# GpSimd's bonus products in two instructions of four heads, and W_in's casts over an even number of outer columns, in a recurrence-and-MLP kernel

## The chip, the cores and the metric

The kernel runs on one core of one Trainium2 chip. The metric is the time of one execution in microseconds on the device, as the median of several runs of the same kernel. TensorE (PE in the profile), VectorE (DVE), ScalarE (ACT) and GpSimd (POOL) compute, each going through its own list of instructions in order; SyncE (SP) issues nearly all DMAs.

## What is computed

A linear recurrence over 768 steps is followed by a two-layer MLP. B = 4, H = 8 heads, S = 768 steps, D = 48 per head, so a token has H*D = 384 numbers, and the hidden layer has 2048.

```python
for t in range(S):
    kt, vt, rt, wt = k[:, :, t], v[:, :, t], r[:, :, t], w[:, :, t]
    cur = np.einsum('bhd,bhe->bhde', u[None] * kt, vt)
    y[:, :, t] = np.einsum('bhd,bhde->bhe', rt, state + cur)
    state = wt[:, :, :, None] * state + np.einsum('bhd,bhe->bhde', kt, vt)
...
x = y.transpose(0, 2, 1, 3).reshape(B * S, H * D)
h = x @ w_in
return np.maximum(0.01 * h, h) @ w_out
```

The part of `cur` that concerns us is the bonus: for each token and head, the sum over d of r*u*k is one number, and it multiplies the token's v.

## The kernel before, in words

The 3072 tokens are cut into 24 chunks of 128 tokens (`NCH`; tokens lie on the 128 partitions), 6 chunks for each batch. The chunks of a batch hang together through the state; the MLP of a chunk needs only that chunk's y. Chunks 0 to 3 go in two pairs (`pair`, L537), the others one by one (`single`, L714).

For each chunk the four inputs w, k, r, v (128 x 384, f32) are loaded into a buffer of the ring `in` (L516). ACT takes the logarithm of w (`lw`, L383), TensorE sums it over time (`cp`, L737), DVE adds to it (`ci`, L752), and ACT takes exponentials (`ek` and, in place, `cp`, L393). The products `rk` (k*ek and r*exp(cp), bf16) are made by DVE or POOL through the helper `times` at L334. They are turned to `rkT`: by TensorE and a copy up to chunk 11 (L441, copies at L329 and L331), by a DMA transpose from chunk 12 on (`TDMA`, L431). TensorE multiplies them to scores `se`, `so` (L787), DVE masks them (`m`, L459), TensorE makes `yp` from m and v (L822) and from the scaled state `sb` (L817). The state `s` is DVE's sum (L479) of `sb`, a product through L334, and of TensorE's outer products of k and v (L640 for pairs, L798).

The bonus (`bonus`, L402 to L421) has four steps: `ru` = r*u, `ru` = ru*k (both mostly on POOL, L334), a sum over each head on DVE to `dg` with 8 numbers for a token (L416), and `vs` = v*dg, in which each number is spread over its head's 48 columns. This last product is 128 x 384 f32 in one instruction of 8 heads, on POOL for 19 chunks and on DVE for 5 (L334 again). `vs` is read in one place: `finish` (L490), where DVE adds it to yp and gives `y`. y goes to `xT`, by TensorE and a copy (L504) or by a DMA transpose (L496).

The MLP of a chunk: TensorE multiplies W_in's 384 x 2048 and xT in four steps of 12 matmuls into `hp` (L860), ACT applies the leaky ReLU and writes `g` (L907), TensorE multiplies g and W_out into `op` in four steps of four matmuls (L928), ACT or DVE copies it to `o` (L329 or L331), and SP stores it (L968).

The weights come as f32 and are cast to bf16 on chip once (`weight_steps`, L349). W_in comes in four buffers, each in two halves: three blocks of 128 rows (t) by 256 columns, so that the f32 half is one contiguous run of 768 for each partition, and its place in `w_in_b` is three runs of 256, 2048 apart. W_out likewise comes in four buffers of two halves, whose place is four runs of 192. Each half is one DMA on SP (L363) and one cast (`copy`, L327: ACT at L329, DVE and POOL at L331). Five of W_in's eight casts are on ACT, two on POOL and one on DVE; of W_out's, two are on ACT, four on POOL and two on DVE.

All steps are recorded with an estimated duration and dependencies (`step`, L317; class `Plan`). A list written out by hand (`EARLY`, L162) gives every step its rank and, by a letter, for some steps another engine (a, v, p for ACT, DVE, POOL). For each compute engine the listed steps also depend on the one ranked before them on that engine, so that the order on each engine stands as written (L972 to L984). The step's function gets the chosen engine as its argument `e`. `P0` is ten times the chunk's number, so `P0 >= 120` means chunk 12 and later.

Of the kernel before, what the change touches and what calls it, by code (L numbers as in the profile page):

```python
# [126 lines left out]
def kernel(  # L127
# [12 lines left out]
    B, H, S, D = r.shape  # L140
# [19 lines left out]
    CASTS = 21  # L160
# [103 lines left out]
    with tc.manual_schedule():  # L264
# [29 lines left out]
        for q in (0, 64):  # L294
            for i, op in ((slice(0, 64), ALU.is_gt), (slice(64, 128), ALU.is_gt),
                          (slice(128, 192), ALU.is_ge), (slice(192, 256), ALU.is_gt)):
                t = pmask[q : q + 64].rearrange("p a t -> p (a t)")[:, i]
# [19 lines left out]
        def step(eng, dur, fn, pri, reads=(), writes=(), deps=(), wire=None, rows=0, **alts):  # L317

            d = list(deps)
            for x in writes:  # L320
                d += x.old
            i = plan.add(eng, dur, fn, d, pri, wire, rows, {eng: dur, **alts} if alts else None)
            for x in (*reads, *writes):
                x.steps.append(i)
            return i

        def copy(e, o, i):  # L327
            if e == "ACT":
                nc.scalar.copy(out=o, in_=i)  # L329
            else:  # L330
                (nc.vector if e == "DVE" else nc.gpsimd).tensor_copy(out=o, in_=i)  # L331

        def times(e, o, a, b):
            (nc.vector if e == "DVE" else nc.gpsimd).tensor_tensor(out=o, in0=a, in1=b, op=ALU.mult)  # L334
# [10 lines left out]
        win_s, wout_s = [], []  # L345
        JQ = NJ // NQ


        def weight_steps(q, which, pri):  # L349
            st = in_r.take()  # L350

            made = []
            for half in range(2):
                part = st.t[:, half * 768 : (half + 1) * 768].rearrange("p (t f) -> p t f", t=(KT, JQ)[which])
                if which == 0:
                    f0 = q * 512 + half * 256
                    src, dst = w_in_v[:, :, f0 : f0 + 256], w_in_b[:, :, f0 : f0 + 256]
                else:
                    n0 = half * DM // 2
                    src = w_out_v[:, q * JQ : (q + 1) * JQ, n0 : n0 + DM // 2]  # L360
                    dst = w_out_b[:, q * JQ : (q + 1) * JQ, n0 : n0 + DM // 2]
                ld = step(
                    "SP", 0.45, lambda part=part, src=src: nc.sync.dma_start(out=part, in_=src), pri,  # L363
                    writes=[st], wire=WWIRE[which], rows=(384, 512)[which])
                made.append(step(
                    ("DVE", "ACT")[half], (0.8, 0.84)[half],
                    lambda e, dst=dst, part=part: copy(e, dst, part), CASTS, reads=[st], deps=[ld],
                    DVE=0.8, ACT=0.84, POOL=1.2))
            (win_s if which == 0 else wout_s).append(made)

# [25 lines left out]
        def product(rk, a, xn, e, P0, deps, banked):  # L396
# [2 lines left out]
                lambda eng: times(eng, rk.t[:, a, :, 0:D], xn.t, e.t[:]),  # L399
                P0, reads=[xn, e], writes=[rk], deps=deps, **({"DVE": 0.58} if banked else {"POOL": 1.05}))  # L400

        def bonus(vs, rn, kn, vn, loads, P0):  # L402

            ru, dg = ru_r.take(), dg_r.take()
            kl, rl, vl = loads
            s_ru = step(
                "POOL", 1.05,
                lambda e: times(e, ru.t[:], rn.t, ubv),
                P0 + 2, reads=[rn], writes=[ru], deps=[rl, u_ld], DVE=0.84)
            s_ruk = step(  # L410
                "POOL", 1.05,
                lambda e: times(e, ru.t[:], ru.t[:], kn.t),
                P0 + 2, reads=[kn, ru], deps=[kl, s_ru], DVE=0.84)
            s_dg = step(
                "DVE", 0.54,
                lambda: nc.vector.tensor_reduce(out=dg.t[:], in_=ru.t[:], axis=AX.X, op=ALU.add),  # L416
                P0 + 2, reads=[ru], writes=[dg], deps=[s_ruk])
            return step(
                "POOL", 0.92,
                lambda e: times(e, vs.t[:], vn.t, dg.t[:].unsqueeze(2).to_broadcast([128, H, D])),  # L420
                P0 + 2, reads=[vn, dg], writes=[vs], deps=[vl, s_dg], DVE=0.84)  # L421

        def gt(t):
# [108 lines left out]
        def weights_at(n):  # L532
            for i, (at, pri) in enumerate(WEIGHTS):
                if n == at:
                    weight_steps(i % NQ, i // NQ, pri)

        def pair(n):  # L537
# [89 lines left out]
            for j in range(2):  # L627
                s_T += turn(rk[j], rkT[j], s_d[j], n, P0, (hp_r, hp_r) if j and n == 0 else (se_r, so_r))
            vs = [vs_r.take() for _ in range(2)]
            s_vs = [bonus(vs[j], rn[j], kn[j], vn[j], (kl, rl, vl), P0) for j in range(2)]  # L630


# [81 lines left out]
        def single(n):  # L714
# [48 lines left out]
            s_T = turn(rk, rkT, [s_r, s_k], n, P0, (se_r, so_r))  # L763
            vs = vs_r.take()
            s_vs = bonus(vs, rn, kn, vn, (kl, rl, vl), P0)


# [115 lines left out]
        for nb in range(4, len(blocks) + 1):  # L883
            a = made[nb][0] if nb < len(blocks) else []
# [12 lines left out]
        for rank, (kind, nb, item) in enumerate(seq):  # L897
            pri = 1000 + rank
            if kind == 0:
                up, j, J, N, g, m_chs, deps = item  # L900
# [17 lines left out]
            else:  # L918
# [12 lines left out]
                deps = [g_done[nb, j] for j in range(q * NJ // 4, (q + 1) * NJ // 4)]  # L931
                deps += wout_s[q * NJ // 4 // JQ] + ([downs[ch]] if q else [])
                if (ch, q) == (NCH - 1, 3):

                    for part, (t, n0, n1) in enumerate(last_parts(op)):
                        o = o_r.take()
# [23 lines left out]
                if q == 3:  # L960
                    o = o_r.take()
                    s_o = step(
                        *(("ACT", 0.5) if ch < OACT else ("DVE", 0.56)),
                        lambda e, o=o, op=op: copy(e, o.t[:], op.t[:, 0:DM]),
# [11 lines left out]
        for rank, word in enumerate(EARLY.split()):  # L976
            i = int(word.rstrip("avp"))
# [50 lines left out]
```

## Time and profile before

| | us |
|---|---|
| median of 5 runs | 186.16 |
| lowest and highest of them | 185.93 and 186.78 |
| the profiled execution's own time | 186.78 |
| its span, first to last instruction | 184.7 |
| TensorE busy | 176.1 (95%) |
| TensorE's weight loads busy | 137.2 (74%) |
| DVE, ACT, POOL busy | 121.2, 121.3, 93.0 |
| `vs` on POOL | 19 instructions, 16.1 in all |
| `vs` on DVE | 5 instructions, 3.0 in all |
| W_in's casts: ACT, POOL, DVE | 0.832 (5), 0.824 (2), 0.953 (1) each |
| W_out's casts: ACT, POOL, DVE | 0.832 (2), 0.824 (4), 0.560 (2) each |

The profile is of one execution. A line of a group gives the source line, the engine, the operation, what it writes and reads, the number of instructions, their busy time and the mean of one in ns, then how long the engine sat idle just before them and what ended that idle time. A line of a timeline gives the start and the duration in us. "PEld" is TensorE's weight load, which overlaps its matmuls. Matmuls are pipelined: a matmul of 128 columns is shown with 219 ns, though they follow each other much more closely. All products of `times` have the line L334, and so are told apart by the names of their tiles.

### The profile page before, as it was taken

What the parts mean: (1) busy time and instruction counts of PE and PEld (TensorE: products, weight loads), DVE (VectorE), ACT (ScalarE), POOL (GpSimd) and SP (SyncE); (2) the same over time, 40 slices, a digit from 0 to 9 for tenths busy, and PEclk for the clock granted to TensorE, in tenths of its full rate; (3) what the DMA queues carried; (4) which work ended last, traced back from release to release, by engine and by line L of the source; (5) the groups of instructions that cost most, each with busy time, mean ns of one, the idle gap of its engine ahead of it and who ended that gap; (6) DMA issues with size and microseconds to landing.
All of it is one profiled execution on the core that took longest, in us unless ns stands there. A gap on an engine that the chain in (4) does not pass through costs nothing.

```text
span 184.7 us, 6227 instructions
## 1 busy us (share of the span) xinstructions
PE 176.1 (95%) x2579; PEld 137.2 (74%) x2583; DVE 121.2 (66%) x237; ACT 121.3 (66%) x263; POOL 93.0 (50%) x129
## 2 busy tenths in 40 slices
PE   7987799999999999999999999999999999999992
PEld 2465587777788697788687787886978777877882
DVE  2488585358678877987868778658548588755000
ACT  2784966665786987798958586666557646652660
POOL 7987582552466778889165656313516256110000
PEclk9999999999999999999999999999999999999999
DMA  6999999988989998996885998888986998941202
GB/s 146 261 282 316 348 330 277 250 172 204 222 166 245 196 230 197 229 217 140 172 159 109 118 199 180 206 163 158 191 203 146 200 197 216 152 108 39 66 4 85
DMA packets 120238, 34.62 MB, mean 187 GB/s; under 512 B 109841, under 2 KB 120210, under 8 KB 120210
## 3 DMA queue, kind: packets, MB, share of 16 engines
q1 hardware_dynamic: 120208, 34.22, 84.1%
q8 instruction: 20, 0.33, 0.8%
q14 instruction: 8, 0.07, 0.1%
q10 hardware_dynamic: 2, 0.00, 0.0%
HBM read 25.17 MB, written 4.72 MB: 162 GB/s over the span
## 4 chain that ended last, share of the span: by engine, by line
PE 77%; SPq 10%; DMA 8%; POOL 2%; issue 1%; DVE 0%
PE op L928 31%; PE hp L860 31%; SPq L516 5%; SPq L363 5%; DMA in<-in_moe_w_in_dram 5%; DMA in<-in_moe_w_out_dram 3%; PE se L787 3%; PE yp L822 2%; PE cp L737 2%; PE yp L817 2%; PE yp L798 2%; PE so L441 1%; PE se L441 1%; PE yp L504 1%; PE cp L742 1%
## 5 line engine op out<-in xcount | busy, mean ns | idle before, releaser
L907 ACT ACTIVATE g<-hp 128x512 bf16<-128x512 f32 x96 | 56.7, 596 | 35.8 <-PE hp L860 33.9
L860 PE MATMUL hp<-xT,w_in_b 128*128 128x128 bf16 x1152 | 76.2, 219 | 1.5 <-ACT w_in_b L329 0.9
L860 PEld LDWEIGHTS <-w_in_b 128*128 128x128 bf16 x1152 | 67.4, 98 | 6.5 <-ACT w_in_b L329 1.2
L928 PE MATMUL op<-w_out_b,g 128*128 128x384 bf16 (+1 forms) x380 | 71.4, 324 | 0.2 <-DVE w_out_b L331 0.2
L928 PEld LDWEIGHTS <-g 128*128 128x128 bf16 x392 | 34.9, 98 | 17.7 <-DVE w_out_b L331 0.3
L334 POOL TENSOR_TENSOR ru<-in,ub 128x384 f32<-128x384 f32 x19 | 19.0, 1007 | 11.7 <-DMA in<-in_r_dram 8.4
L334 POOL TENSOR_TENSOR rk<-in,ek 128x384 bf16<-128x384 f32 x15 | 15.2, 1011 | 17.0 <-ACT ek L393 15.6
L334 POOL TENSOR_TENSOR vs<-in,dg 128x384 f32<-128x384 f32 x19 | 16.1, 852 | 14.5 <-DVE dg L416 11.3
L490 DVE TENSOR_TENSOR y<-yp,vs 128x384 bf16<-128x384 f32 x24 | 13.3, 555 | 13.0 <-PE yp L822 9.5
L334 POOL TENSOR_TENSOR ru<-ru,in 128x384 f32<-128x384 f32 x15 | 15.5, 1042 | 4.1 <-DMA in<-in_k_dram 2.5
L334 POOL TENSOR_TENSOR sb<-s,a 128x384 bf16<-128x384 f32 x13 | 11.3, 867 | 11.7 <-DVE s L479 4.4
L459 DVE TENSOR_TENSOR m<-se,maskb 128x512 bf16<-128x512 f32 x20 | 13.7, 685 | 3.6 <-PE so L787 3.3
L459 DVE TENSOR_TENSOR m<-so,maskb 128x512 bf16<-128x512 f32 x20 | 13.7, 685 | 3.5 <-PE so L787 3.5
L383 ACT ACTIVATE lw<-in 128x384 bf16<-128x384 f32 x24 | 12.3, 520 | 3.1 <-DMA in<-in_w_dram 3.1
L752 DVE TENSOR_TENSOR ci<-cp,lw 128x384 f32<-128x384 f32 x20 | 11.1, 553 | 4.3 <-PE cp L742 3.9
L334 DVE TENSOR_TENSOR rk<-in,cp 128x384 bf16<-128x384 f32 x22 | 12.1, 548 | 2.6 <-ACT cp L393 2.1
L416 DVE TENSOR_REDUCE dg<-ru 128x8 f32<-128x384 f32 x24 | 13.0, 545 | 0.2
L329 ACT COPY o<-op 128x384 f32<-128x384 f32 (+1 forms) x16 | 7.5, 470 | 6.5 <-PE op L928 5.1
L479 DVE TENSOR_TENSOR s<-yp,sb 128x384 f32<-128x384 f32 x14 | 7.8, 554 | 5.2 <-PE yp L798 5.2
L393 ACT ACTIVATE cp<-cp 128x384 f32<-128x384 f32 x22 | 10.5, 479 | 0.6 <-DVE ci L752 0.3
L393 ACT ACTIVATE ek<-ci 128x384 f32<-128x384 f32 x20 | 10.4, 518 | 0.4 <-DVE ci L752 0.2
L441 PEld LDWEIGHTS <-rk 128*128 128x128 bf16 x96 | 6.6, 103 | 2.4 <-DVE rk L334 1.0
(125 smaller groups left out, 222.9 us busy)
## 6 DMA issues: line engine op xcount, KB each, us to landing
out_dram<-o SPq DMA_DIRECT2D x23, 192.0 KB, 2.9
in<-in_w_dram SPq DMA_DIRECT2D x20, 192.0 KB, 4.1
in<-in_r_dram SPq DMA_DIRECT2D x20, 192.0 KB, 3.7
in<-in_k_dram SPq DMA_DIRECT2D x20, 192.0 KB, 3.9
in<-in_v_dram SPq DMA_DIRECT2D x20, 192.0 KB, 3.7
in<-in_moe_w_in_dram SPq DMA_DIRECT2D x8, 384.0 KB, 7.7
in<-in_moe_w_out_dram SPq DMA_DIRECT2D x8, 384.0 KB, 7.4
in<-in_w_dram SPq DMA_DIRECT2D x2, 384.0 KB, 5.0
```

The costliest lines, as they stand in the source:

```text
L334: (nc.vector if e == "DVE" else nc.gpsimd).tensor_tensor(out=o, in0=a, in1=b, op=ALU.mult)
L363: "SP", 0.45, lambda part=part, src=src: nc.sync.dma_start(out=part, in_=src), pri,
L383: lambda: nc.scalar.activation(out=lw.t[:, :, 0:D], in_=wn.t, func=AF.Ln),
L393: "ACT", 0.5, lambda: nc.scalar.activation(out=out.t[:], in_=i, func=AF.Exp, scale=scale),
L416: lambda: nc.vector.tensor_reduce(out=dg.t[:], in_=ru.t[:], axis=AX.X, op=ALU.add),
L441: nc.tensor.transpose(trv[:, g, :], rk.t[:, a, 2 * g : 2 * g + 2, :].rearrange("p h d -> p (h d)"), ident[:])
L459: lambda par=par: nc.vector.tensor_tensor(out=m.t[:, par], in0=gt(sc[par].t), in1=mask.unsqueeze(1).to_broadcast([128, NP, 128]), op=ALU.m ...
L490: lambda: nc.vector.tensor_tensor(out=y.t[:], in0=hd(yp.t[:, 0:DM]), in1=vs.t[:], op=ALU.add),
L752: lambda: nc.vector.tensor_tensor(out=ci.t[:], in0=hd(cp.t[:, 0:DM]), in1=lw.t[:, :, 0:D], op=ALU.add),
L860: nc.tensor.matmul(hp.t[:, a * N : (a + 1) * N], lhsT=w_in_b[:, t, (j + a) * 128 : (j + a + 1) * 128], rhs=xT[:, t, c0 : c0 + N], start=(a ...
L907: lambda hp=hp, g=g, j=j, J=J, N=N: nc.scalar.activation(out=g.t[:, j : j + J, 0:N], in_=hp.t[:, 0 : J * N].rearrange("p (a n) -> p a n", ...
L928: nc.tensor.matmul(t[:, 0 : n1 - n0], lhsT=g.t[:, j, off : off + 128], rhs=w_out_b[:, j, n0:n1], start=(j == 0), stop=(j == NJ - 1))
```

## The change

Two independent edits. In `weight_steps`, the cast of a half of W_in is given another view of the same elements: each run of 256 columns is split in two halves of 128, and the half (a) becomes the outermost dimension, so that source and destination both have 2 x 3 rows of 128 in place of one run of 768 and three rows of 256. All eight casts of W_in are affected, on whichever engine they are; W_out's are left as they were. In `bonus`, where the last product is on POOL and the chunk is 12 or later, it is made in two instructions of four heads (128 x 192) each, one after the other. These are nine of the nineteen on POOL, those of chunks 12, 14, 16 and 18 to 23. On every engine the order of the instructions is otherwise the same.

```diff
+        def even(t, which):
+
+            return t if which else t.rearrange("p t (a f) -> p a t f", a=2)
...
-                    lambda e, dst=dst, part=part: copy(e, dst, part), CASTS, reads=[st], deps=[ld],
+                    lambda e, dst=even(dst, which), part=even(part, which): copy(e, dst, part), CASTS, reads=[st], deps=[ld],
...
+        def by_heads(e, o, a, b, parts):
+            for i in range(parts):
+                hs = slice(i * H // parts, (i + 1) * H // parts)
+                times(e, o[:, hs, :], a[:, hs, :], b[:, hs].unsqueeze(2).to_broadcast([128, H // parts, D]))
...
-                lambda e: times(e, vs.t[:], vn.t, dg.t[:].unsqueeze(2).to_broadcast([128, H, D])),
+                lambda e: by_heads(e, vs.t, vn.t, dg.t, 2 if e == "POOL" and P0 >= 120 else 1),
```

## The prediction, as it was made before the changed kernel ran

> **What bounds the kernel now.** I read the page first: the 40 slices say where each engine is full.
>
> ```profile
> PE 176.1 (95%) x2579; PEld 137.2 (74%) x2583; DVE 121.2 (66%) x237; ACT 121.3 (66%) x263; POOL 93.0 (50%) x129
> ...
> PE   7987799999999999999999999999999999999992
> ...
> DMA  6999999988989998996885998888986998941202
> ```
>
> TensorE is at 9 from slice 8 on (a slice is 184.7 / 40 = 4.62 us); before that the DMA row is full and TensorE isn't. So there are two stages, and I cut the span at 40.4 us, where the chain of waits becomes TensorE alone, and asked for busy times by window:
>
> ```profile
> 18.00:40.40 22.40, 20.20 (x393) 16.37 (x387) 13.43 (x25) 15.27 (x28) 12.89 (x16) 1.00 1.01 279
> 40.40:181.40 141.00, 141.00 (x1983) 112.41 (x1981) 96.29 (x178) 95.16 (x211) 65.75 (x74) 1.00 0.81 168
> ```
>
> The columns are the window and its length, then PE, PEld, DVE, ACT, POOL with counts, then clock, DMA share, GB/s. In the second window TensorE is busy for all 141.00 of 141.00 us. Asked who waited for whom from 40.5 to 181.4 us, TensorE has no entry at all. A busy TensorE need not be at its peak, but nothing here waits for DVE, ACT or POOL. From 18 to 40.5 us it has these:
>
> ```profile
> PE hp L860 <- ACT w_in_b L329: 0.9, 2, 0.6
> PE so L441 <- POOL rk L334: 0.5, 1, 0.5
> PE hp L860 <- ACT g L907: 0.4, 1, 0.4
> PE op L928 <- DVE w_out_b L331: 0.2, 1, 0.2
> ```
>
> (total us, times, longest): 2.0 us together. The reader should notice what isn't there: DVE's cast of W_in. The last of these waits, the 0.5 at about 40 us, is what fixes where the full stage begins, and the chain shows what it hangs on:
>
> ```profile
> 31.39 6.39 DMA in<-in_moe_w_out_dram
> 37.78 0.05 issue
> 37.84 0.57 POOL w_out_b L331
> 38.41 0.43 issue
> 38.83 1.10 POOL rk L334
> 39.94 0.05 issue
> 39.98 0.40 PE so L441 x4
> ```
>
> The last piece of W_out lands at 37.78; POOL, idle 1.46 us before, casts it, forms rk, and TensorE goes on at 39.98. The front is paced by the weights' arrival, and the SP queue that issues those loads goes by the DMA engines (share 1.01), not by the engines of this change. The loads into reused buffers that also wait for POOL or DVE (25.49 and 28.97 us) wait for products of chunks 0 and 1, done by 14 us.
>
> [...] a cast of 768 elements whose destination has 4 outer columns against one of 3:
>
> ```profile
> 20.79 0.95 DVE L331 CAST w_in_b<-in 128x768 bf16<-128x768 f32 x1 [1.70 <-DMA in<-in_moe_w_in_dram]
> 21.66 0.41 DVE L331 COPY rkT<-so 128x512 bf16<-128x512 bf16 x1
> ...
> 28.92 0.56 DVE L331 CAST w_out_b<-in 128x768 bf16<-128x768 f32 x1 [1.64 <-DMA in<-in_moe_w_out_dram]
> ```
>
> [...] DVE's sb at 23.38, started under POOL's cast of 23.07 to 23.89, took 0.92 in place of 0.55. [...] POOL's casts give the size: 822 ns for 768 elements, 502 for 384, so 0.83 ns an element and about 0.18 us fixed.
>
> **Part 1, the casts of W_in.** There are eight: five on ACT (832 ns), two on POOL (824), one on DVE (953). Same elements, now in 2x3 rows of 128; the order on every engine is unchanged.
> DVE: 953 becomes 560, the row of the 4-column cast: 0.39 us less. [...] The rkT copy behind it reads transposes issued at 20.90, so it can follow. TensorE's outer products, which wait for that copy, stand behind twelve hp matmuls of 21.41 to 22.1 that wait for an xT copy on ACT. There is no DVE wait in TensorE's list to remove, and POOL is idle from 20.97 to 23.07[...]. DVE's next blocked op, sb at 23.38, stays held by POOL's cast, which the DMA starts. On the path: 0.
> ACT and POOL: the number of rows has cost nothing so far: POOL casts to 4 columns and to 3 both take 822 to 827, and rk written in 8 rows takes 997 like ru written in one. I take 0. As no row shows this form, I keep both ends, 0.2 us less or more per cast (an estimate: POOL's fixed part). ACT's casts stand before TensorE twice in series (0.9 and, through g, 0.4), each restarted by a DMA landing. 0.2 more would meet the covers of 0.2 at L928 and 0.5 at L441 that wait for W_out anyhow; 0.2 less would lengthen these waits. On the path: 0. If that cover were gone, 0.2 to 0.4.
>
> **Part 2, POOL's bonus products.** Nine vs products from chunk 12 on (86.65 to 158.97 us, mean 833 ns) become eighteen of 192 elements. Each pair costs at least what one does now (same elements; I see no reason for a gain) and at most twice that, 0.83 more, as half can't cost more than the whole. I take the fixed part, 0.18 more: 1.01 a pair, 1.6 us of POOL in all. POOL is at 65.75 of 141 us there. After them come waits: six of the nine are followed by an idle gap of 0.45 to 3.9 us; behind the others (86.65, 130.68, 152.64) stands one ru product and then a gap of 4.41, 3.17 and 1.43.
> Who reads vs: only DVE's y, in order of chunk. The last four, counted back from the last y: vs ends 153.47, 157.00, 159.80 against y at 160.00, 166.54, 170.26, and 142.85 against 151.36. The least slack is 6.5 us. y itself waits for TensorE (9.5 us in 12 waits), never for vs.
> [...] The busiest place is this:
>
> ```profile
> 152.64 0.83 POOL L334 TENSOR_TENSOR vs<-in,dg 128x384 f32<-128x384 f32 x1
> 153.43 1.31 POOL L334 TENSOR_TENSOR ru<-ru,in 128x384 f32<-128x384 f32 x1
> 156.17 0.83 POOL L334 TENSOR_TENSOR vs<-in,dg 128x384 f32<-128x384 f32 x1 [1.43 <-DVE dg L416]
> ```
>
> DVE's ru (153.13) and rk (154.27, ends 155.15) alternate with them. rk is what matters: SP issues its transpose at 156.10, 0.95 later, and it lands 5.1 us after, 161.2, for scores on TensorE just before 162.89. A delay of 0.18 + 0.55 = 0.73 is inside the first 0.95. On the path: 0.
>
> **Sum.** The profiled execution took 186.78 (span 184.70, 2.08 around it). 186.78 + 0 + 0 = 186.78, no change. Against the median of the five, 186.16, it is the slowest of them, so I carry the change, 0, to the median: 186.2.
>
> **Rivals.**
> A, the front shortens: all of DVE's 0.39 reaches the end, 186.16 - 0.39 = 185.8, and at most the 2.0 us of TensorE's waits, 184.2; a middle case takes the 0.9 of the two waits for ACT's casts, 185.3. For it: W_in's casts are in that list. Against: [...] L441 waits for W_out at 37.78 in any case.
> B, slower: POOL and DVE hold each other up at 152.6 to 157. If each of the four halves takes 0.83 and then waits one DVE op of 0.55, the two pairs take 4 x 1.38 = 5.52 in place of 1.66, 3.9 late. It decides from the point where rk's transposes are late for the scores: 0.95 at SP plus 1.4 after landing (161.2 to about 162.6), 2.3 in all. 3.9 - 2.3 = 1.6, so 187.8; half of that, 187.0, if only part of it meets rk. Against: it needs the upper bound everywhere.
> C, it doesn't do what it says: the cast stays at 0.95[...]. 186.2 too, since nothing waited for it.
>
> **The numbers.** A difference under 0.3%, 0.56 us, is about what a measurement of this kernel can tell from no change. Forecast 0.66 and C 0.06, both within; A 0.16, of which 0.11 beyond 0.56; B 0.12, of which 0.11 beyond. Faster 0.11, same 0.66 + 0.06 + 0.05 + 0.01 = 0.78, slower 0.11. The five runs spread from 185.93 to 186.78; with the 0.4 that casts could cost and part of A (185.5) and B (186.9), the range is 185.5 to 186.9.
>
> **What would show it.** Right: DVE's cast near 0.56 (apart from a wait), each vs pair near 1.0 by its starts, TensorE without waits from 40.4 on, L441 still held by POOL's rk behind the last W_out cast. Wrong: ACT's or POOL's W_in casts off 0.83; an entry of TensorE waiting for L787's rkT or for sb after 86 us (B); the full stage beginning well before or after 40 us (A).

## The result and the profile after

| | before | after |
|---|---|---|
| median, us | 186.16 (49 runs) | 186.53 (27 runs) |
| lowest to highest | 185.78 to 186.97 | 186.21 to 187.15 |
| ratio to before, 95% interval | | 1.0016 [1.0009, 1.0023] |
| the profiled execution's time and span | 186.78, 184.7 | 186.21, 184.2 |

The forecast was 186.2 us, range 185.5 to 186.9, most likely no difference beyond 0.3%. The time is in the range and the difference is 0.16%. But the interval excludes zero: about 0.3 us (0.0016 x 186.16) is there for which the prediction's sum has no term. The ratio is taken from all runs of both kernels at their usual speed, not from the two medians, so it differs a little from the ratio of these; of the ratios below, e1's leaves out one far-off run of e1 (440.54 us), and those of e1 to e4 one of before (238.56 us). The two profiled executions can't show it by their lengths, since before's was the slowest of its first five and after's the fastest of its runs.

First the page of after, the rows that the prediction showed for before:

```profile
PE 176.3 (96%) x2579; PEld 137.5 (75%) x2583; DVE 122.7 (67%) x237; ACT 121.4 (66%) x263; POOL 94.8 (51%) x138
...
PE   7988899999999999999999999999999999999992
...
DMA  6999999999979899987784997888989997641202
```

The same two stages. POOL has nine instructions more (138 against 129) and 1.8 us more of work. Next the busy time by window of after (columns as in the prediction):

```profile
18.00:40.40 22.40, 20.87 (x405) 17.03 (x399) 14.13 (x26) 15.54 (x29) 13.46 (x16) 1.00 1.07 290
40.40:181.40 141.00, 140.17 (x1975) 111.81 (x1972) 97.43 (x179) 94.93 (x211) 67.28 (x82) 1.00 0.81 166
```

TensorE ends at 180.57 here, so 140.17 is all of the time from 40.40 on. Asked for TensorE's waits, the trace of after has no entry from 40.5 to 181.4 us, and these from 18 to 40.5 us:

```profile
PE hp L869 <- ACT w_in_b L329: 0.6, 1, 0.6
PE hp L869 <- ACT g L916: 0.4, 1, 0.4
PE op L937 <- ACT g L916: 0.2, 1, 0.2
```

(The lines are nine or four further on: L860 is now L869, L928 is L937, L441 is L450.) The wait for POOL's `rk` is gone in this execution. The last casts of W_out show why, in a timeline of after:

```profile
36.79 0.82 POOL L331 CAST w_out_b<-in 128x768 bf16<-128x768 f32 x1 [0.57 <-DMA in<-in_moe_w_out_dram]
...
37.85 1.04 POOL L334 TENSOR_TENSOR rk<-in,ek 128x384 bf16<-128x384 f32 x1 [0.24 <-issue]
```

The cast began at 36.79, where before's began at 37.84, so `rk` was ready before TensorE wanted it. That is the DMA's doing, as the bracket says, and not the changed casts': in the profiles of after and of eight experiments below (e1 to e7 and e10) this cast began between 36.65 and 37.40, whether W_in's casts were changed or not, and TensorE waited for `rk` in one of the nine (e4, 0.4 us). The execution of before that was profiled, with 37.84, is the exception.

Laid beside each other instruction by instruction, after's TensorE runs ahead of before's by 0.85 us from 40.4 us on, and stays so, within 0.01 us, up to the last matmul. These are the last lines of TensorE's timeline, before's and then after's:

```profile
181.03 0.39 PE L940 MATMUL yp<-w_out_b,g 128*128 128x128 bf16 x4
```

```profile
180.18 0.39 PE L949 MATMUL yp<-w_out_b,g 128*128 128x128 bf16 x4
```

Each line merges four matmuls that are shown with 219 ns each; they start 0.06 us apart: (0.39 - 0.219) / 3. 181.03 - 180.18 is 0.85, yet the spans differ by 0.49 only. So some 0.36 us has come in **behind TensorE's last matmul**. What is left there is the last result's copy and store, and the closing barrier, which is POOL's last seven entries: a semaphore that is reached once the rest is done (POOL stands idle for 20.4 us before it), a second one that lets the other engines go on, an instruction named Drain, a clearing of semaphores, a second Drain and two more semaphores. These are POOL's entries in the groups of the barrier's line, before's (from 183.9 us) and then after's (from 183.0 to 183.6, and from 183.6 us); the columns are the number, then the shortest, median and longest in ns, then the first and last start:

```profile
L1023 POOLq EVENT_SEMAPHORE  x2: 17/17/17, 184.0 to 184.1; - x2
...
L1023 POOLq DRAIN  x2: 34/56/78, 184.2 to 184.4; - x2
```

```profile
L1032 POOLq EVENT_SEMAPHORE  x2: 17/17/17, 183.1 to 183.5; - x2
...
L1032 POOLq DRAIN  x2: 34/87/140, 183.6 to 183.9; - x2
```

The two semaphores follow each other by 0.1 us before and by 0.4 after. The trace has 183.994 and 184.078 before, an idle gap of 0.067 us between them, and 183.148 and 183.523 after, a gap of 0.358. The first Drain behind them takes 140 ns in place of 78. Together 0.29 + 0.06 = 0.35 us, and the other engines' release, which comes 0.04 to 0.05 us after POOL's second semaphore in both, is as late.

### The profile page after: what moved, and what is told of

It is laid out like the page before. It is cut to its first block, busy times and chain, and to the rows that moved or that the text cites. A ratio compares the mean times of both kernels' runs of the same rounds, so it can differ in the third digit from the quotient of the medians.

```text
span 184.2 us, 6236 instructions
## 1 busy us (share of the span) xinstructions
PE 176.3 (96%) x2579; PEld 137.5 (75%) x2583; DVE 122.7 (67%) x237; ACT 121.4 (66%) x263; POOL 94.8 (51%) x138
## 4 chain that ended last, share of the span: by engine, by line
PE 82%; SPq 10%; DMA 5%; ACT 1%; issue 0%; DVE 0%
PE op L937 34%; PE hp L869 33%; SPq L367 5%; DMA in<-in_moe_w_out_dram 5%; SPq L525 4%; PE se L796 3%; PE yp L831 2%; PE cp L746 2%; PE yp L826 2%; PE yp L807 2%; PE yp L513 1%; PE se L450 1%; PE so L450 1%; PE cp L751 1%; ACT g L916 1%
## 5 line engine op out<-in xcount | busy, mean ns | idle before, releaser
L869 PE MATMUL hp<-xT,w_in_b 128*128 128x128 bf16 x1152 | 76.2, 219 | 1.2 <-ACT w_in_b L329 0.6
L869 PEld LDWEIGHTS <-w_in_b 128*128 128x128 bf16 x1152 | 67.4, 98 | 6.2 <-ACT w_in_b L329 1.0
L937 PE MATMUL op<-w_out_b,g 128*128 128x384 bf16 (+1 forms) x380 | 71.4, 325 | 0.2 <-ACT g L916 0.2
L937 PEld LDWEIGHTS <-g 128*128 128x128 bf16 x392 | 34.8, 98 | 17.8 <-DVE w_out_b L331 0.3
L334 POOL TENSOR_TENSOR vs<-in,dg 128x192 f32<-128x192 f32 (+1 forms) x28 | 18.1, 663 | 13.8 <-DVE dg L425 10.4
L450 PEld LDWEIGHTS <-rk 128*128 128x128 bf16 x96 | 6.9, 105 | 1.4 <-DVE rk L334 0.7
```

Source lines behind the costliest of these rows:

```text
L450: nc.tensor.transpose(trv[:, g, :], rk.t[:, a, 2 * g : 2 * g + 2, :].rearrange("p h d -> p (h d)"), ident[:])
L869: nc.tensor.matmul(hp.t[:, a * N : (a + 1) * N], lhsT=w_in_b[:, t, (j + a) * 128 : (j + a + 1) * 128], rhs=xT[:, t, c0 : c0 + N], start=(a ...
L937: nc.tensor.matmul(t[:, 0 : n1 - n0], lhsT=g.t[:, j, off : off + 128], rhs=w_out_b[:, j, n0:n1], start=(j == 0), stop=(j == NJ - 1))
```

## The experiments

**Theory "end":** the changed parts cost nothing; nine more entries in POOL's list move a place of that list, at which POOL stalls for 0.3 us, into the closing barrier. **Rival "front":** W_in's casts act on the front. **Rival "middle":** the split products hold up TensorE. The first four kernels ran beside the same runs of before.

**e1_casts_only** has only the casts' edit, **e2_split_only** only the products'. Their diffs are the two halves of the diff above.

> The eight casts of W_in in the changed form, the bonus products in one instruction each. Theory (the end): the added time sits after the last matmul, in POOL's part of the closing barrier, because POOL's list of instructions is nine longer; here it has the length of before, so the ratio is 1.000 and the gap between POOL's two closing semaphore instructions is about 0.08 us. Rival (the front): [...] then the ratio is 1.001 to 1.002 here.

> The nine bonus products in two instructions each, the casts as before. Theory (the end): 1.0016, with a gap of about 0.37 us between POOL's two closing semaphore instructions, and no wait of TensorE after 40.5 us. Rival (the front): 1.000. Second rival (the middle): POOL's extra 0.14 us per pair reaches TensorE somewhere after 86 us; then 1.0016 too, but with waits of TensorE there.

Measured: e1 186.27 us, ratio 0.9994 [0.9984, 1.0005]; e2 186.48, 1.0011 [1.0001, 1.0021]. In e1 POOL's closing gap is 0.067 us and the Drain 78 ns, in e2 0.358 and 140, to the nanosecond as in after. So what is lost belongs to the split. "Front" falls.

**e3_nine_more** is the kernel before with nothing changed but nine tiny instructions on POOL, behind its last product and some 20 us before the end. **e4_after_plus_twenty** is the changed kernel with twenty of them.

```diff
+        for _ in range(9):
+            nc.gpsimd.memset(pa_r.tiles[0][:, 0, 0, :], 0.0)
```

> The kernel before, with nine small memsets of a scratch tile added behind POOL's last product, some 18 us ahead of the end; no cast and no product is changed. Theory (the end): 1.0016 and the gap of 0.37 us at POOL's closing barrier, since only the number of POOL's instructions counts. Both rivals: 1.000.

> The changed kernel, with twenty small memsets added behind POOL's last product. Theory (the end), if the stall stands at a certain place of POOL's list: the place now falls among the memsets, where nobody waits, so 1.000 with a gap of 0.08 us at the barrier. If the stall comes from any longer list: 1.0016 or more. Both rivals: 1.0016, as for the changed kernel.

Measured: e3 186.56 us, 1.0021 [1.0011, 1.0031], gap 0.358 and Drain 140 ns; e4 186.0 us, 0.9993 [0.9981, 1.0005], gap 0.066 and 78 ns. Nine instructions that nobody waits for cost what the split costs, and more of them on top of the split take the cost away. "Middle" falls with it: e3 has no split products. POOL's barrier entries in e3, up to the first Drain:

```profile
L1025 POOLq EVENT_SEMAPHORE  x2: 17/17/17, 183.4 to 183.8; - x2
L1025 POOLq DRAIN  x1: 140/140/140, 183.9 to 183.9; - x1
```

**A fixed place, or any longer list?** The next kernels add other numbers of the same instruction: **e5_after_plus_one** one to the changed kernel (ten more than before), **e6_six_more** six and **e10_three_more** three to the kernel before. Diffs as above, with 1, 6 and 3 for 9.

> The changed kernel with one more small memset at the end of GpSimd's own work: ten instructions more than the kernel before, where the change has nine. Theory (one place in GpSimd's list stalls, and only when a waiting instruction doesn't cover it): the place moves onto the wait of the closing barrier, the gap between GpSimd's two closing semaphores is back at 0.07 us and the last Drain at 0.078 us, ratio to the kernel before 1.000 (0.999 to 1.001). Rival (every list that is nine or more longer pays at the end, until the next place is reached): gap 0.36 us, ratio 1.0016 to 1.002.

> The kernel before with six small memsets at the end of GpSimd's own work. Theory (a fixed place in the list): the place falls some instructions later, among the last ones of the closing barrier; a stall of about 0.3 us is then seen at a later instruction than with nine, with the gap between the two closing semaphores at 0.07 us; ratio 1.0015 to 1.002 if all wait for that instruction, 1.000 if nobody does. Rival (six more instructions just cost their own time): ratio 1.000, no stall anywhere, since they end long before TensorE does.

> The kernel before with three small memsets at the end of GpSimd's own work. Theory (the stall belongs to one place of GpSimd's list, which this list ends before): no stall in the closing barrier, gap 0.07 us, ratio 1.000 (0.999 to 1.001). Rival (each instruction more at the end costs some tens of ns, so that three cost a third of what nine do): ratio 1.0005 to 1.0008.

Measured: e5 186.09 us, 0.9992 [0.9982, 1.0002], gap 0.069; e6 186.51, 1.0017 [1.0008, 1.0026]; e10 186.39, 1.0017 [1.0007, 1.0027]. In e6 the two semaphores are 0.066 us apart, and the stall stands three entries further on, between the barrier's range clear and its second Drain. These are e6's entries from 183.5 to 184.1 us:

```profile
L1025 POOLq EVENT_SEMAPHORE_RANGE_CLEAR  x1: 94/94/94, 183.5 to 183.5; - x1
L1025 POOLq DRAIN  x1: 183/183/183, 183.9 to 183.9; - x1
```

From the clear's end to the Drain is 0.323 us (before 0.034), and the Drain takes 183 ns (before 34). Of e10 the theory said "no stall" and 1.000, and **missed**: 1.0017. Its span is no longer at all, and POOL's barrier looks as before. The answer is outside the span. The difference between a run's time and its span is known for every run:

| kernel | POOL's entries more than before | the list's entry 196 | gap before that entry, us | span, median us | time less span, mean us | ratio |
|---|---|---|---|---|---|---|
| before | 0 | not in the trace (its list ends at 192) | | 184.1 | 2.12 | 1 |
| e10 | 3 | the next after its last (195) | not in the trace | 183.9 | 2.50 | 1.0017 |
| e6 | 6 | barrier's second Drain | 0.323 | 184.5 | 2.04 | 1.0017 |
| after, e2, e3 | 9 | barrier's second semaphore | 0.358 | 184.5, 184.4, 184.5 | 2.05, 2.06, 2.06 | 1.0016, 1.0011, 1.0021 |
| e5 | 10 | barrier's first semaphore, a wait of 20 us | hidden in it | 184.0 | 2.06 | 0.9992 |
| e4 | 29 | an added instruction | 0.057, as its neighbours | 184.0 | 2.05 | 0.9993 |
| e7 (below) | 63 | the last part of a split product, at 132 us | none | 184.05 | 2.04 | 0.9994 |

I counted POOL's entries in the trace in order of their starts, from 0, semaphores included. With six, nine and ten more the entry that stalls, or would, is the same one, number 196. With three more the list ends at 195, and 0.38 us appears behind the last entry that the trace has, where 196 would come. So "a fixed place" stands, and the miss of e10 only extends it by one position beyond the traced end. Where 196 is the entry that waits for the last store, or lies among instructions that end early, nothing is lost.

The traces hold a second sign of this place. Each has, after the span's start, nine transfers of 8 KB of the kind "instruction" on DMA queue 14. Eight of them come at the same times in all kernels, to 2 us (in e9 up to 5 us later). The ninth moves with POOL's list. In after, e2, e3 and e6 it starts 0.70 to 0.71 us behind the start of entry 196, just outside the span. In e5, e4 and e7 it starts at 164.7, 161.2 and 132.6 us, so their profile pages, which count what falls within the span, have one more. This is the line in the pages of before and after, and then in e5's:

```profile
q14 instruction: 8, 0.07, 0.1%
```

```profile
q14 instruction: 9, 0.07, 0.1%
```

In e10 it starts 1.07 us behind the end of POOL's last entry. Less the 0.71, that leaves 0.36 us: the gap of 0.358, where entry 196 would come. In before it starts 1.8 us behind the last entry, so before meets the place too, outside its span. Its time less span, 2.12, is 0.06 to 0.08 above that of the kernels that meet the place earlier, so some of the cost may stand in before's own time; that isn't shown.

The place has a forerunner 128 entries earlier. POOL's entry 68 is the `rk` of the front's last gate. In eleven of the twelve profiles (in e9 the order there is another) it starts 0.44 to 0.46 us after the semaphore in front of it, where the next such pair is 0.10 us apart (0.14 in after). The profile names nothing that it waited for; its input `ek` had been written at 35.88 in before, and `rk` started at 38.83. A transfer of 8 KB starts 0.9 to 1.9 us later, with the DMA engines busy (in before at 39.92, with a DMA share of 1.17 from 39 to 40 us). In before this is the line "38.41 0.43 issue" of the chain that the prediction shows, with the cast's end at 38.66 inside it, so that 0.18 is left as an idle gap.

**e7_eight_parts** tests "middle" at a much larger dose: 2 becomes 8 in the split, one head in each instruction.

```diff
-                lambda e: by_heads(e, vs.t, vn.t, dg.t, 2 if e == "POOL" and P0 >= 120 else 1),
+                lambda e: by_heads(e, vs.t, vn.t, dg.t, 8 if e == "POOL" and P0 >= 120 else 1),
```

> The changed kernel with each of the nine bonus products in eight instructions of one head each, in place of two of four: 54 more on GpSimd than the change has. Theory (the prediction's slack of over 6 us of these products, and the place in the list moved into the body): the product takes 1.8 to 2.3 us in place of 0.97, no TensorE wait after 40.5 us, closing gap 0.07 us, ratio 1.000 (0.999 to 1.001). Rival (the split delays TensorE through late products): waits of op or of a y matmul on GpSimd's products after 85 us, ratio 1.003 or more.

Measured: 186.12 us, 0.9994 [0.9981, 1.0007], no entry of TensorE from 40.5 us on, gap 0.066. A timeline of POOL in e7, the product that the prediction priced at 1.01 in two parts:

```profile
86.10 1.84 POOL L334 TENSOR_TENSOR vs<-in,dg 128x48 f32<-128x48 f32 x8
87.90 1.00 POOL L334 TENSOR_TENSOR ru<-ru,in 128x384 f32<-128x384 f32 x1
```

It takes 1.80 us from start to start, 1.0 more than before; the nine products grow by 1.0 to 2.0 us each, and nothing is late. So the slack of these products was real and large, and the cost was never one of work.

**e8_cast_twice** and **e9_cast_four_times** test the other step of the prediction, that DVE's cast of W_in is off the path. In the kernel before, that one cast is issued twice or four times over the same block.

```diff
-                    lambda e, dst=dst, part=part: copy(e, dst, part), CASTS, reads=[st], deps=[ld],
+                    lambda e, dst=dst, part=part, times_=2 if which == 0 and q == 1 and half == 0 else 1: [copy(e, dst, part) for _ in range(times_)], CASTS, reads=[st], deps=[ld],
```

> The kernel before with VectorE's one cast of W_in issued twice over the same block: about 0.95 us more on VectorE at 21 us, where the change takes 0.4 us away. Theory (the front is covered by the waits that come after it, for the gate's input and for the last W_out block): a new or longer wait of hp near 22 us, shorter ones after it, the last wait before 40 us ending where it did; ratio 1.000 (0.999 to 1.001). Rival (VectorE's cast is on the path to the end): 0.5 to 0.95 us longer, ratio 1.003 to 1.005.

> The kernel before with VectorE's one cast of W_in issued four times over the same block: about 2.86 us more on VectorE at 21 us. Theory (a later VectorE is taken up by the waits after it only up to some 0.4 to 0.9 us, the rest goes to the end): a wait of the route's matmuls near 22 us of 2.5 us or so, and 1.5 to 2.3 us more in all, ratio 1.008 to 1.012. Rival (the stretch up to 40 us is paced by the transfers of W_out alone, so that VectorE's casts don't count at all): ratio under 1.003.

Measured: e8 186.41 us, 1.0012 [1.0001, 1.0023]; e9 190.47, 1.0218 [1.0196, 1.024]. TensorE's waits up to 40.5 us in e8, and up to 42 us in e9:

```profile
PE so L640 <- DVE rkT L331: 0.7, 1, 0.7
PE hp L860 <- ACT w_in_b L329: 0.6, 1, 0.6
```

```profile
PE so L640 <- DVE rkT L331: 2.7, 1, 2.7
PE hp L860 <- ACT w_in_b L329: 0.9, 2, 0.6
```

In both a wait for DVE's `rkT` copy appears near 22 us, and the waits for `g`, for W_out's cast and for `rk` are gone. In e8 that pays for most of it: 0.95 more on DVE, 0.7 of it seen by TensorE, 0.2 (0.0 to 0.4) at the end. Its 1.0012 is just above the theory's 0.999 to 1.001, though the interval reaches into it, and far below the rival's 1.003. In e9 **both sides missed**, at 1.008 to 1.012 and under 1.003: 2.86 more on DVE cost 4.3 us. The windows of e9 show what was not reckoned with, in the last column but two, TensorE's granted clock as a share of its full speed:

```profile
22.00:24.00 2.00, 0.28 (x4) 0.10 (x2) 1.93 (x3) 1.15 (x2) 0.82 (x1) 0.89 1.06 341
24.00:26.00 2.00, 1.01 (x18) 0.86 (x18) 1.55 (x4) 0.00 (x0) 1.35 (x2) 0.50 1.10 327
26.00:28.00 2.00, 2.00 (x21) 1.94 (x19) 1.86 (x3) 0.60 (x1) 1.13 (x2) 0.50 1.11 327
28.00:30.00 2.00, 2.00 (x27) 1.80 (x28) 1.30 (x3) 1.29 (x3) 0.59 (x1) 0.50 1.14 290
30.00:32.00 2.00, 1.99 (x57) 1.81 (x58) 1.43 (x3) 1.26 (x4) 1.01 (x2) 0.91 1.06 257
```

By these windows the granted clock was 0.50 for about 6.8 us in all, from the end of the window 22 to 24 on (an estimate: 2 x 0.11 / 0.5 in the first of these windows, 2 in each of the next three, 2 x 0.09 / 0.5 in the last). The first 1.4 us of it lie in the wait itself, which ends at 24.99 by the timeline, and cost nothing more. Of the other 5.4 us I take half as lost, 2.7, plus the wait's 2.7: 5.4. The old waits, 2.0 us in before's profile with 0.9 of them kept, take up 1.1 of it. That leaves 4.3 by this estimate, and 4.3 us reached the end. The clock fell some 1.3 us into the wait, which began at 22.27. In e8, whose longest wait from 18 us on was 0.7, the mean granted clock of the profiled execution was 1.0. How long a wait must be for the clock to fall, and when it rises again, isn't shown by these two.

## Why the prediction was right, and what it missed

**Two stages, TensorE the bound from 40 us on: right.** After has no TensorE wait in the second stage, and its TensorE instructions keep step with before's to 0.01 us all through it.

**The last gate at 40 us, behind W_out's landing: right for the execution it was read from, too firm as a rule.** The wait for `rk` is 0.5 in before's profile, 0.4 in e4's, and absent in the eight others without added casts. So one of the signs that were named for "right", L441 held by `rk`, did not appear in after. One profile can't tell a gate that is always last from one that is last at times.

**DVE's cast, "953 becomes 560": right where POOL was idle.** These are after's lines around it, from a timeline:

```profile
20.33 0.99 POOL L334 TENSOR_TENSOR ru<-in,ub 128x384 f32<-128x384 f32 x1
...
20.65 1.09 DVE L331 CAST w_in_b<-in 128x768 bf16<-128x768 f32 x1 [1.52 <-DMA in<-in_moe_w_in_dram]
...
21.66 0.41 DVE L331 COPY rkT<-so 128x512 bf16<-128x512 bf16 x1
```

The product `ru` ends at 21.32, and the cast at 21.74, 0.42 later: most of its 1.09 is waiting. After's cast of W_out at 35.50 did the same under POOL's `sb`, which ended at 36.22: it took 1.13 and ended 0.41 later. Before's cast, which took 0.95, ended at 21.74 as well, so of the gain of 0.39 us nothing is there. Where POOL happened to be done (e1, its `ru` ended at 20.58 and the cast began at 20.67) the cast took 0.56, as the row of the 4-column cast had promised. So the form does what was forecast, and POOL's product took the gain back. Shown are these times; what in the form makes the cast shorter, and why it waits for POOL, isn't.

**"On the path: 0" for the casts: right for the change, and held in one direction only.** e1 gives -0.1 us (-0.3 to +0.1). In the other direction e8 shows the cover to be thin, some 0.7 of 0.95, and e9 shows it gone. **ACT's and POOL's casts at 0 more: right**, as after's groups of `w_in_b` from 18 to 30 us show:

```profile
L329 ACT CAST w_in_b<-in x4: 832/832/832, 18.4 to 25.1; 128x768 bf16<-128x768 f32 x4
L331 POOL CAST w_in_b<-in x2: 824/828/831, 22.9 to 24.0; 128x768 bf16<-128x768 f32 x2
L331 DVE CAST w_in_b<-in x1: 1087/1087/1087, 20.7 to 20.7; 128x768 bf16<-128x768 f32 x1
```

**0.18 more for a split product: nearly right.** Undisturbed it is 0.14. By POOL's timeline, before and then after:

```profile
86.65 0.83 POOL L334 TENSOR_TENSOR vs<-in,dg 128x384 f32<-128x384 f32 x1
87.44 1.00 POOL L334 TENSOR_TENSOR ru<-ru,in 128x384 f32<-128x384 f32 x1
```

```profile
85.80 0.97 POOL L334 TENSOR_TENSOR vs<-in,dg 128x192 f32<-128x192 f32 x2
86.73 1.00 POOL L334 TENSOR_TENSOR ru<-ru,in 128x384 f32<-128x384 f32 x1
...
151.94 1.29 POOL L334 TENSOR_TENSOR vs<-in,dg 128x192 f32<-128x192 f32 x2
153.19 0.99 POOL L334 TENSOR_TENSOR ru<-ru,in 128x384 f32<-128x384 f32 x1
```

From start to start, 0.79 became 0.93. In the busiest place the pair took 1.25, 0.32 more again; the prediction allowed 0.55 for a DVE instruction in between, an estimate of its author from the length of one. **The slack of 6.5 us and more: right**, e7 used 1.0 to 2.0 of it.

**The sum, "186.78 + 0 + 0": a term was missing.** It priced the nine added instructions by their durations and by who waits for them, and on the path both are nothing. It did not ask where they push the instructions behind them. The closing barrier stands at the end of POOL's list, it is on the path whatever POOL did before, and the nine entries moved the stalling entry 196 into it: 0.35 us in the profile, 0.3 by the ratio. With one or twenty idle instructions more, which take that entry out of the way, the changed kernel gives 0.9992 and 0.9993 (e5, e4), and both intervals hold the forecast's 0. So the forecast of no difference beyond 0.3% was right, and so were its reasons for both edits; it was low by this term. That a difference of 0.16% stays below 0.3% was no merit of the sum, which had no place for it. The same stall stood, without a price, in the chain that the prediction shows, as the 0.43 us of "issue" in front of `rk`.

**Rivals.** A (front shortens) would be 0.4 or 0.9 us below before; e1's interval leaves at most 0.3. B (POOL and DVE hold each other up, 187.0 or 187.8) did not occur. C did half occur, since the cast took 1.09 us in after and its gain was waited away, and that was worth nothing, as said.

**What stays open.** Why entry 196 stalls isn't shown. What the traces have beside it is this: two delays of about 0.3 us at entries 128 apart, each with a transfer behind it that the profile calls "instruction" and that has 8 KB. Whether the transfer has to do with the stall isn't shown, nor what POOL does in that time: in after the transfer starts 0.71 us after the stall has ended, so the stall isn't a wait for its data. Nor does the trace say why e4's transfer starts 2.2 us before entry 196 does, and there that entry doesn't stall. Shown are the place, the size, that the number of POOL's entries decides, and that an instruction transfer moves with that number.

None of these kernels beats the one before beyond what the measurement can tell; e5, e4 and e7 come nearest, at 0.9992 to 0.9994.

## What to carry to other kernels

When an edit adds instructions to an engine, ask also what stands at the end of that engine's list and who waits for it there: a few entries more or less can be worth 0.3 us though none of them is on the path. A difference of that size should be tested with idle instructions on the same engine before it is put down to the edit, and the time outside the span should be compared as well as the span. And cover is a stock: on the same engine 0.4 us less work gained nothing here, 0.95 us more cost 0.2, and 2.9 us more cost 4.3, with TensorE's granted clock at 0.50 for some 6.8 us of it.

## What the runs showed of the hardware

- POOL stalled at one entry of its list: 0.29 us more of idle gap, and the Drain behind it or at it 0.06 or 0.15 us longer, in four kernels inside the closing barrier and in a fifth (0.38 us) behind the span. Another entry, 128 places earlier, came 0.34 us later behind its semaphore than the next such pair in most of eleven profiles. A transfer of 8 KB of the kind "instruction" started 0.70 to 0.71 us behind the first place in those four kernels, and 0.9 to 1.9 us behind the second.
- With a wait of TensorE of 2.7 us its granted clock was 0.50 for some 6.8 us (an estimate from windows of 2 us), from about 1.3 us after the wait's start (e9); with one of 0.7 us the mean granted clock was 1.0 (e8).
- DVE's cast of 768 elements in 2 x 3 rows of 128 took 0.56 us when POOL was idle (e1), and 1.09 when POOL's product still had 0.67 us to run (after); in the form of before it took 0.95 (e8, e9: 952 to 954 ns, six times).
- A product of 384 elements on POOL cost 0.79 us from start to start in one instruction, 0.93 in two and 1.80 in eight: about 0.14 us for each instruction more.
